# Exponentials of a scale and of its double in one ScalarE operation, from a pair (2 alpha, alpha) that GpSimd writes into the buffer of P

## Chip, cores and metric

The kernel runs on one core of one Trainium2 chip. The metric is the device time of one execution in microseconds; the time of the kernel before is the median of three runs. The profile is of one execution, whose own time is given beside its span.

## What is computed

Two independent parts share the core, and their outputs stand side by side in 1280 columns. Part A is a dilated sliding attention over 2048 positions (32 heads, a window of 8 positions with a step of 2) with its projections. Part B is a state space convolution: a kernel K is made from 640 x 192 complex exponents and convolved with u by FFT.

```python
dt = jnp.exp(log_dt)[:, None]
A = A_re + 1j * A_im
logdA = dt * A
dB = dt * Bc
P = jnp.exp(logdA[:, :, None] * l[None, None, :])          # l = 0 .. 2047
K = jnp.einsum("dn,dnl,dn->dl", Cc, P, dB).real
...
Yf = Uf * Kf[None, :, :, :]                                 # FFT of length 2 L
y = irfft2(Yf) + u * Dskip
```

The change touches only the real part of the exponents: exp(m x alpha) with alpha = dt x A_re, for the multipliers m that the tables need.

## The kernel before

**Tables.** The 640 channels are worked off in five chunks of 128 (`NCH`). In a chunk, P is not made for all 2048 positions l: l is split as 64 x j + 8 x b + a, and exponentials are made for a (0 to 7), 8 b (0 to 56) and 64 j (0 to 31). These are 48 places `e` in the table R (128 partitions, 48 x `NE_R` = 48 x 4 numbers in bf16): places 0 to 7 hold a, 8 to 15 hold 8 b, 16 to 31 hold 64 j for j from 16 to 31, and 32 to 47 hold 64 j for j from 15 down to 0. `R_MULT` (L55) lists the multipliers. In `exps_chunk` (L213 to L223) GpSimd writes ones to the three places with m = 0 (L217, L218), and ScalarE makes the other 45 with one operation each (L222): 192 numbers of alpha in f32, times the scale m, through Exp, to 4 neighbouring numbers in each of 48 groups. R has two buffers, R0 and R1, for even and odd chunks.

The phases come from `trig_half` (L226), once per half chunk: TensorE makes them in PSUM (ps_ph, L247 and L250), and ScalarE takes the sine (L255) into the tables TA and TX. Exp and Sin need different tables of ScalarE, so a table load stands at each turn from one to the other.

**Products.** `small_half` (L265) runs on VectorE, all at L271 but for one scaling at L286. It writes P (a product of R and TA), Q (P times the coefficients cT), F, G, and two tiles X. P and Q are there to make F; after Q is written nothing reads P. P, F and G have one buffer each; Q and the following Y share four buffers with the tag Y. `y_form` (L296) makes Y from F and G, three for each of the two units of a half chunk (L305), and `kgen_unit` (L309) multiplies X and Y on TensorE into ps_k (L318, L323), which ScalarE copies to Ksb (L324).

**FFT.** `fwd` (L327) transforms in two stages on TensorE (ps_f, L337 and L343), with a copy by ScalarE after each of their four parts (A at L338, Sg at L344). It runs for u (`fwd_u`) and for K of the chunk before (`transform`). `products` (L348) multiplies both spectra on VectorE (L358), and `inverse_a` goes back (Z, L375).

**Order.** Every engine works its instructions in program order; a scheduler merges the operations that the functions of `body` (L662) issue into one order per engine, and `keep_in_program_order` and `issue_after` tie some of them. In the loop over chunks (L719) the order of ScalarE from chunk to chunk is: TA and TX of the second half, the coefficients of the next chunk (L206, L207), a table load, the 45 exponentials of the next chunk with copies (Ksb, Z, A, Sg) in between, a table load, TA and TX of the next chunk's first half. From chunk 0 to 1 all 45 stand ahead of A and Sg of `fwd_u`; from 1 to 2 the last 31 stand behind Sg; from 2 to 3 the last 18, and from 3 to 4 the last 12. P of the next chunk waits for its TA. In chunk 0 the exponentials follow right after alpha (L155, fill of chunk 0), beside VectorE's preparation of the phases (L175 to L193). Pools named `prep_...` exist only in this preparation; `tabb` holds P, F, G, X, Y and UD.

GpSimd has little to do: ones into R, descriptors for some loads, and at the start two operations on the coefficients (L209, L210) and a copy (L694). Later it copies a few columns of kT (L481).

Of the kernel before, what the change touches and what calls it, by code (L numbers as in the profile page):

```python
# [10 lines left out]
A = mybir.AluOpType  # L11
ACT = mybir.ActivationFunctionType
AX = mybir.AxisListType
bf16 = mybir.dt.bfloat16
f32 = mybir.dt.float32
# [36 lines left out]
    return F1, F64  # L52


R_MULT = [float(a) for a in range(8)] + [8.0 * b for b in range(8)] + [64.0 * (16 + i) for i in range(16)] + [64.0 * (31 - i) for i in range(16, 32)]  # L55
L1_OF_ROW = [16 + i for i in range(16)] + [31 - i for i in range(16, 32)]


# [23 lines left out]
def inline(nc, arr, name):  # L82
    return nc.inline_tensor(np.ascontiguousarray(arr).astype(np.float32).astype(ml_dtypes.bfloat16), name=name).ap()
# [118 lines left out]
def coefficients(engine, B, c):  # L202

    co = B["cT"][:, c]
    if engine.engine == mybir.EngineType.Activation:
        engine.activation(out=co[:, :, 1], in_=co[:, :, 2], func=ACT.Copy, scale=-1.0)  # L206
        engine.copy(out=co[:, :, 3], in_=co[:, :, 0])  # L207
    else:
        engine.tensor_scalar(out=co[:, :, 1], in0=co[:, :, 2], scalar1=-1.0, scalar2=None, op0=A.mult)  # L209
        engine.tensor_copy(out=co[:, :, 3], in_=co[:, :, 0])  # L210


def exps_chunk(tc, pools, B, c):  # L213
    nc = tc.nc
    R = pools["tab"].tile([128, 48, NE_R, 4], bf16, name="R", tag=f"R{c % 2}")
    src = B["alpha"][:, c].rearrange("p u (q f) -> p (u q) f", f=4)
    nc.gpsimd.memset(R[:, :, 0:16:8, :], 1.0)  # L217
    nc.gpsimd.memset(R[:, :, 47, :], 1.0)  # L218
    for e, m in enumerate(R_MULT):
        if m == 0.0:  # L220
            continue
        nc.scalar.activation(out=R[:, :, e, :], in_=src, func=ACT.Exp, scale=m)  # L222
    return R  # L223


# [122 lines left out]
def products(tc, pools, Sk, Sd, pool, late):  # L348

    nc = tc.nc  # L350
    P1 = pool.tile([128, 32, 32, 4], bf16, name="P1", tag="sp", bufs=3)
    P2 = pool.tile([128, 32, 32, 4], bf16, name="P2", tag="sp", bufs=3)
    fl = lambda t: t.rearrange("p a b c -> p (a b c)")
    nc.sync.dma_start(out=fl(P1[:]), in_=Sd)
    nc.sync.dma_start(out=fl(P2[0:64]), in_=Sd[64:128])
    nc.sync.dma_start(out=fl(P2[64:128]), in_=Sd[0:64])
    for P in (P1, P2):
        ins = nc.vector.tensor_tensor(out=P[:], in0=P[:], in1=Sk[:], op=A.mult)  # L358
        if late:
            tc.keep_in_program_order(ins)  # L360
    return P1, P2, ins


def inverse_a(tc, pools, C, P1, P2, Zd, pool):

    nc = tc.nc
    MM = nc.tensor.matmul
    Z = pool.tile([128, 128, 32], bf16, name="Z", tag="sp", bufs=3)

    def piece(b):  # L370
        ps = pools["psum"].tile([128, 8, 128], f32, name="ps_ia", tag="bank2")
        for j in range(8):
            for w, P in enumerate((P1, P2)):
                MM(ps[:, j], lhsT=P[:, 8 * b + j].rearrange("p k g -> p (k g)"), rhs=C["EA"][:, w, :], start=(j % 4 == 0 and w == 0), stop=(w == 1), skip_group_check=True)
        nc.scalar.copy(out=Z[:, :, 8 * b:8 * b + 8], in_=ps[:].rearrange("p j x -> p x j"))  # L375
        if b == 3:
            nc.sync.dma_start(out=Zd, in_=Z[:].rearrange("p x j -> p (x j)"))

    return [lambda b=b: piece(b) for b in range(4)]
# [11 lines left out]
def fwd_u(tc, pools, C, Sd, c):  # L391

    U = C["U"][:].rearrange("p l (ut c) -> p c l ut", c=NCH)[:, c]
    Su, last = fwd(tc, pools, C, (lambda ut: U[:, :, ut]), 0, pools["fft"])
    tc.nc.sync.dma_start(out=Sd[c], in_=Su[:].rearrange("p a b c -> p (a b c)"))
    return last
# [265 lines left out]
def body(tc, ctx, pools, prm, B_u, B_Dskip, Sd, Zd, UDd, A_x, A_wqkv, A_wo, out_a, out_b):  # L662
    nc = tc.nc
# [12 lines left out]
    R, trig = {}, {}  # L676
    with tc.tile_pool(name="prep_b", bufs=1) as pb, tc.tile_pool(name="prep_c", bufs=1) as pc, tc.tile_pool(name="prep_a", bufs=1) as pa, tc.tile_pool(name="psum_p", bufs=2, space=bass.MemoryType.PSUM) as psp:
        pools.update(prep_a=pa, prep_b=pb, prep_c=pc)
        B, fill = partB_prep(tc, dict(pools, psum=psp), prm)
        fill(0, 1, lambda u: None)  # L680
        Dn = pa.tile([128, 160], bf16, name="Dn")
        dsrc = B_Dskip.rearrange("(g ch) -> g ch", g=4)
        late = tc.keep_in_program_order
        late(nc.sync.dma_start(out=BD[:].rearrange("p a b n -> p (a b n)"), in_=inline(nc, cn["BD"], "c_BD")))
        late(nc.sync.dma_start(out=EA[:].rearrange("p a n -> p (a n)"), in_=inline(nc, cn["EA"], "c_EA")))
        late(nc.sync.dma_start(out=T2[:].rearrange("p a n -> p (a n)"), in_=inline(nc, cn["T2"], "c_T2")))
        for g in range(4):
            late(nc.sync.dma_start(out=Dn[32 * g:32 * g + 32, :], in_=dsrc[g].partition_broadcast(32)))
        coefficients(nc.gpsimd, B, 0)
        R[0] = exps_chunk(tc, pools, B, 0)  # L690
        trig[0, 0] = trig_half(tc, pools, B, 0, 0)
        usrc = B_u[0].rearrange("(l1 l0) (g ch) -> g l1 l0 ch", l0=64, g=4)
        fill(1, NCH, lambda g: late(nc.sync.dma_start(out=U[32 * g:32 * g + 32], in_=usrc[g])))
        nc.gpsimd.tensor_copy(out=Dsb[:], in_=Dn[:].rearrange("p (ut c) -> p c ut", c=NCH))  # L694
# [5 lines left out]
    def transform(c):  # L700
        Sk[c] = fwd(tc, pools, C, (lambda ut: Kb[c][:, ut, :]), 1, fp)[0]

    def unit(c, h, uu, F, G, X, between=lambda: None):
        Ys = [y_form(tc, pools, F, G, uu, k) for k in range(3)]
        between()
        kgen_unit(tc, dict(pools, psum=psg), 2 * h + uu, X, Ys, Kb[c])
        if 4 * c + 2 * h + uu in UD_AFTER:
            times_d(tc, pools, C, UDd, *divmod(UD_AFTER.index(4 * c + 2 * h + uu), 2))
# [10 lines left out]
    for c in range(NCH):  # L719
        Kb[c] = (fp, pools["tabb"])[c % 2].tile([128, 32, 64], bf16, name="Ksb", tag="Ksb")  # L720
        F, G, Xs = small_half(tc, pools, B["cT"][:, c], R[c], *trig[c, 0][:2], 0)
        if c > 0:
            transform(c - 1)
        trig[c, 1] = trig_half(tc, pools, B, c, 1)
        unit(c, 0, 0, F, G, Xs[0])
        if c > 0:
            P1, P2, last = products(tc, pools, Sk[c - 1], Sd[c - 1], fp, True)
            ia = inverse_a(tc, pools, C, P1, P2, Zd[c - 1], fp)
            ia[0]()
        unit(c, 0, 1, F, G, Xs[1])  # L730
        if c > 0:
            for f in ia[1:]:
                f()
        if c < LAST:
            last_u = fwd_u(tc, pools, C, Sd, c if c == 0 else c + 1)
            if c == 0:
                first_u = last_u
        if c == LAST:
            att.open_k()
            for ct in range(5):  # L740
                att.proj_k(0, ct)
            att.k_halo()
        with ExitStack() as order:
            if c > 0:
                order.enter_context(tc.issue_after(last.ins))
            F, G, Xs = small_half(tc, pools, B["cT"][:, c], R[c], *trig[c, 1][:2], 1)
        if c < LAST:
            with tc.issue_after(trig[c, 1][2].ins):
                coefficients(nc.scalar, B, c + 1)
                R[c + 1] = exps_chunk(tc, pools, B, c + 1)  # L750
            trig[c + 1, 0] = trig_half(tc, pools, B, c + 1, 0)
        else:
            att.open_q0()
        with ExitStack() as order:
            if c == 0:
                order.enter_context(tc.issue_after(first_u.ins))
            unit(c, 1, 0, F, G, Xs[0])
        if c == 0:
            fwd_u(tc, pools, C, Sd, 1)
        unit(c, 1, 1, F, G, Xs[1], q_first if c == LAST else lambda: None)  # L760
        if c == LAST - 1:
            att.load_x()
# [45 lines left out]
    def fill(some, n=1):  # L808
        for f in some[0:n]:
            f()  # L810
        del some[0:n]
# [14 lines left out]
    for i0, ni, j0, nj, done in ((0, 128, 2, 3, 0), (128, 128, 2, 3, 1), (256, 128, 0, 4, None), (256, 256, 4, 1, 2), (384, 128, 0, 4, 3)):  # L826
        for w in range(W):
            att.av_step(i0, ni, j0, nj, w)
            if (done, w) in LOADS:
                qr, c = LOADS[done, w]  # L830
# [16 lines left out]
def kernel(  # L847
# [28 lines left out]
    Zd = dpool.tile([NCH, 128, 4096], bf16, name="Zdram")  # L876
    UDd = dpool.tile([NCH, 128, 2048], bf16, name="UDdram")
    body(tc, ctx, pools, prm, B_u, B_Dskip, Sd, Zd, UDd, A_x, A_wqkv, A_wo, out_a, out_b)


# [28 lines left out]
```

## Time and profile before

| | |
|---|---|
| time, median of 3 runs | 439.51 us (439.4 to 442.8) |
| profiled execution, its own time | 438.98 us |
| its span | 437.2 us |
| PE (matmul) busy | 358.4 us, 82% |
| VectorE (DVE) busy | 391.3 us, 89% |
| ScalarE (ACT) busy | 314.0 us, 72% |
| GpSimd (POOL) busy | 44.5 us, 10% |
| mean granted TensorE clock | 0.916 |
| the 225 exponentials (L222) | 59.3 us busy, mean 358 ns of one |
| the 60 products Y (L305) | 102.9 us busy, mean 1751 ns of one |

In the rows of the profile an operation is given with its line in the kernel, its engine, the tile written and the tiles read ("R<-LPC": alpha lies in the tile LPC), and the shapes in partitions x elements. Operations of one engine overlap a little at their ends, so the mean length of one is more than the distance from one to the next. In a timeline the columns are start, length (both in us, from the start of the span), engine, line, operation, tiles, shapes and count; in brackets stands the idle time of the engine ahead of it and what ended that. In rows by window the columns after the window's length are the busy time and the count of instructions of PE, PE's weight loads, DVE, ACT and POOL, then the granted clock, the DMA share and GB/s.

The chunks end, by the first product P of the next one, at 75.72 (chunk 1 begins), 133.35, 184.28 and 233.99 us.

### The profile page before, as it was taken

What the parts mean: (1) busy time and instruction counts of PE and PEld (TensorE: products, weight loads), DVE (VectorE), ACT (ScalarE), POOL (GpSimd) and SP (SyncE); (2) the same over time, 40 slices, a digit from 0 to 9 for tenths busy, and PEclk for the clock granted to TensorE, in tenths of its full rate; (3) what the DMA queues carried; (4) which work ended last, traced back from release to release, by engine and by line L of the source; (5) the groups of instructions that cost most, each with busy time, mean ns of one, the idle gap of its engine ahead of it and who ended that gap; (6) DMA issues with size and microseconds to landing.
All of it is one profiled execution on the core that took longest, in us unless ns stands there. A gap on an engine that the chain in (4) does not pass through costs nothing.

```text
span 437.2 us, 17687 instructions
## 1 busy us (share of the span) xinstructions
PE 358.4 (82%) x8041; PEld 241.1 (55%) x8041; DVE 391.3 (89%) x386; ACT 314.0 (72%) x570; POOL 44.5 (10%) x85
## 2 busy tenths in 40 slices
PE   1397659989886998879778799999899897399995
PEld 0145546866863677556665665545555674134443
DVE  7889999999997999999999989946978989999751
ACT  3974998889999899979997845342858344544663
POOL 7440000000000000000010000400001204102110
PEclk9996577999999898889999899999999999659999
DMA  5569102163233402324079933500210907957343
GB/s 143 186 141 200 18 3 109 39 227 94 99 123 123 97 28 98 144 103 99 27 258 241 236 75 135 178 0 3 67 32 1 265 17 201 228 141 225 96 107 114
DMA packets 45131, 51.62 MB, mean 118 GB/s; under 512 B 31376, under 2 KB 38992, under 8 KB 42368
## 3 DMA queue, kind: packets, MB, share of 16 engines
q1 hardware_dynamic: 41520, 41.41, 35.4%
q0 software_dynamic: 3392, 8.95, 7.0%
q8 instruction: 63, 1.03, 1.0%
q10 hardware_dynamic: 144, 0.12, 0.1%
q14 instruction: 12, 0.10, 0.1%
HBM read 28.03 MB, written 18.35 MB: 106 GB/s over the span
## 4 chain that ended last, share of the span: by engine, by line
PE 49%; ACT 29%; DVE 14%; issue 5%; DMA 1%; SPq 1%; DVEq 0%; ACTq 0%
ACT R L222 10%; ACT A L338 6%; PE ps_k L318 6%; PE ps_ph L247 6%; PE ps_k L323 6%; PE ps_op L420 6%; PE ps_k L470 4%; PE ps_q L488 4%; PE ps_ph L250 4%; ACT Sg L344 4%; PE ps_f L343 4%; PE ps_v L501 2%; DVE prod L521 2%; ACT Z L375 2%; PE ps_o L420 2%
## 5 line engine op out<-in xcount | busy, mean ns | idle before, releaser
L305 DVE TENSOR_TENSOR Y<-F,G 128x3072 bf16<-128x3072 bf16 x60 | 102.9, 1751 | 0.6 <-PE ps_k L323 0.6
L222 ACT ACTIVATE R<-LPC 128x192 bf16<-128x192 f32 x225 | 59.3, 358 | 0.1
L247 PE MATMUL ps_ph<-LPC 128*128 128x256 bf16 (+1 forms) x200 | 41.5, 311 | 17.3 <-DMA LPC<-lo 8.7
L318 PE MATMUL ps_k<-Y,X 128*32 128x64 bf16 x1920 | 47.2, 239 | 7.3 <-DVE Y L305 3.8
L323 PE MATMUL ps_k<-Y,X 64*32 64x64 bf16 x1920 | 43.8, 233 | 3.4 <-issue 3.3
L344 ACT CAST Sg<-ps_f 128x1024 bf16<-128x1024 f32 x40 | 37.6, 1027 | 7.3 <-PE ps_f L343 7.3
L318 PEld LDWEIGHTS <-X 128*32 128x32 bf16 x1920 | 32.1, 117 | 17.4 <-issue 9.0
L343 PE MATMUL ps_f<-A,T 128*128 128x128 bf16 x320 | 27.3, 259 | 14.9 <-ACT A L338 14.2
L338 ACT CAST A<-ps_f 128x1024 bf16<-128x1024 f32 x40 | 37.6, 1036 | 0.7 <-PE ps_f L337 0.6
L271 DVE TENSOR_TENSOR X<-R,TX 128x1536 bf16<-128x1536 bf16 x40 | 36.4, 951 | 0.0
L323 PEld LDWEIGHTS <-X 64*32 64x32 bf16 x1920 | 29.6, 113 | 12.1 <-issue 4.4
L255 ACT ACTIVATE TX<-ps_ph 128x864 bf16<-128x864 int16 (+1 forms) x40 | 31.9, 867 | 5.3 <-DVE X L271 2.5
L343 PEld LDWEIGHTS <-T 128*128 128x128 bf16 x320 | 25.6, 119 | 16.1 <-issue 14.9
L585 DVE TENSOR_TENSOR prod<-v,atp 128x2048 bf16<-128x2048 bf16 (+2 forms) x32 | 31.3, 1018 | 2.0 <-PE ps_o L420 1.8
L255 ACT ACTIVATE TA<-ps_ph 128x768 bf16<-128x768 int16 x40 | 30.6, 822 | 3.4 <-PE ps_ph L250 3.0
L250 PE MATMUL ps_ph<-LPC 128*64 128x128 bf16 (+1 forms) x400 | 29.6, 249 | 0.0
L247 PEld LDWEIGHTS <-LPC 128*128 128x128 bf16 x200 | 15.0, 102 | 25.9 <-issue 19.1
L420 PE MATMUL ps_op<-wo,o 128*128 128x320 bf16 x160 | 28.5, 315 | 0.8 <-ACT o L595 0.4
L358 DVE TENSOR_TENSOR P<-P,Sg 128x4096 bf16<-128x4096 bf16 x10 | 22.9, 2288 | 4.1 <-DMA P<-Sdram 3.2
L250 PEld LDWEIGHTS <-LPC 128*64 128x64 bf16 x400 | 15.2, 118 | 19.1 <-issue 18.9
L611 ACT CAST ob<-ps_op 128x320 bf16<-128x320 f32 x28 | 11.9, 431 | 19.0 <-PE ps_op L420 17.3
L337 PE MATMUL ps_f<-BD,U 128*64 128x128 bf16 x320 | 19.4, 285 | 6.1 <-ACT A L338 3.3
(129 smaller groups left out, 661.2 us busy)
## 6 DMA issues: line engine op xcount, KB each, us to landing
Sdram<-Sg SPq DMA_DIRECT2D x5, 1024.0 KB
P<-Sdram SPq DMA_DIRECT2D x5, 1024.0 KB
P<-Sdram SPq DMA_DIRECT2D x10, 512.0 KB
Zdram<-Z SPq DMA_DIRECT2D x5, 1024.0 KB
Z<-Zdram SPq DMA_DIRECT2D x30, 128.0 KB
U<-in_B_u_dram SPq DMA_DIRECT2D x4, 640.0 KB
UDdram<-UD SPq DMA_DIRECT2D x10, 256.0 KB
out_dram<-ysb SPq DMA_DIRECT2D x32, 80.0 KB
```

What stands on the lines that cost most here:

```text
L222: nc.scalar.activation(out=R[:, :, e, :], in_=src, func=ACT.Exp, scale=m)
L247: MM(o[:, :, 0:32], lhsT=L[:, 0:128], rhs=rhs, start=first, stop=last, skip_group_check=True)
L250: MM(o[64 * hh:64 * hh + 64, :, 32:48], lhsT=L[:, 128:192], rhs=rhs[:, :, 16 * hh:16 * hh + 16], start=False, stop=last, skip_group_check= ...
L255: last = nc.scalar.activation(out=dst[:, qs, e0:e0 + 2 * n, :].rearrange("p q (b e) f -> p b e q f", b=2), in_=words.rearrange("p b (e q f ...
L271: TT = lambda o, a, b, op: V.tensor_tensor(out=o, in0=a, in1=b, op=op)
L305: nc.vector.tensor_tensor(out=Y[:].rearrange("p q (b a) f -> p q b a f", a=8), in0=fa, in1=gb, op=A.mult)
L318: MM(ps[32 * g:32 * g + 32, t], lhsT=X[:, q, 2 - k, :, f], rhs=Ys[k][:, q, :, f], start=(t == 0 and k == 0), stop=False, tile_position=(0, ...
L323: MM(ps[32 * g:32 * g + 32, t], lhsT=X[hb, q, 2 - k, :, f], rhs=Ys[k][hb, q, :, f], start=False, stop=(k == 2), tile_position=(64 * (g // ...
L338: nc.scalar.copy(out=A1[:, :, 32 * b:32 * b + 32].rearrange("p k (j g) -> p k j g", g=4), in_=ps[:].rearrange("p j k g -> p k j g"))
L343: last = MM(ps[:, kk], lhsT=C["T2"][:, 8 * b + kk, :], rhs=A1[:, 8 * b + kk, :], start=(kk % 4 == 0), stop=True, skip_group_check=True)
L344: nc.scalar.copy(out=Sg[:, :, 8 * b:8 * b + 8, :], in_=ps[:].rearrange("p k (j g) -> p j k g", g=4))
L420: self.MM = lambda *a, **k: self.tc.keep_in_program_order(self.nc.tensor.matmul(*a, **k))
```

## The change

Exponentials of m and 2 m are made by one operation where both are needed. Its input is a pair of tiles, `twice`: 2 alpha and alpha side by side; with the scale m the operation gives exp(2 m alpha) and exp(m alpha) at once, to two places of R. Among 1 to 7 and among 8 to 56 the pairs are (1, 2) and (3, 6), and 4, 5 and 7 times the unit stay single; among 64 to 1984 there are ten pairs and eleven singles. That makes 14 pairs of 384 numbers and 17 singles of 192: 31 operations instead of 45. The singles, which read alpha itself, come first.

`twice` is written by two scalings of 192 f32 numbers each. In chunk 0 VectorE does it, into a tile of the preparation. For the chunks 1 to 4 GpSimd does it, into a tile with the tag of P in `tabb`: after the Q of the second half of the chunk before, and ahead of the P of the next chunk, which waits until the pairs were read. On GpSimd the writes stand ahead of the ones for R. In the merged order the pairs stand: from chunk 0 to 1 all ahead of A and Sg; from 1 to 2 all behind Sg; from 2 to 3 and from 3 to 4 two between A and Sg and twelve behind Sg. The order of the other operations is the same but for small moves; in chunk 0 the two scalings on VectorE stand ahead of the first subtraction of the phases (L179).

```diff
-R_MULT = [float(a) for a in range(8)] + [8.0 * b for b in range(8)] + [64.0 * (16 + i) for i in range(16)] + [64.0 * (31 - i) for i in range(16, 32)]
...
-def exps_chunk(tc, pools, B, c):
+def exps_chunk(tc, pools, B, c, engine, twice):
     nc = tc.nc
     R = pools["tab"].tile([128, 48, NE_R, 4], bf16, name="R", tag=f"R{c % 2}")
-    src = B["alpha"][:, c].rearrange("p u (q f) -> p (u q) f", f=4)
+    alpha = B["alpha"][:, c].rearrange("p u w -> p (u w)")
+    for b in range(2):
+        engine.tensor_scalar(out=twice[:, b], in0=alpha, scalar1=2.0 - b, scalar2=None, op0=A.mult)
     nc.gpsimd.memset(R[:, :, 0:16:8, :], 1.0)
     nc.gpsimd.memset(R[:, :, 47, :], 1.0)
-    for e, m in enumerate(R_MULT):
-        if m == 0.0:
-            continue
-        nc.scalar.activation(out=R[:, :, e, :], in_=src, func=ACT.Exp, scale=m)
+    one, two = [], []
+    for places in ({a: a for a in range(1, 8)}, {8 * a: 8 + a for a in range(1, 8)}, {64 * j: j if j > 15 else 47 - j for j in range(1, 32)}):
+        left = sorted(places)
+        while left:
+            m = left.pop(0)
+            e, step = places[m], 0
+            if 2 * m in left:
+                left.remove(2 * m)
+                step = places[2 * m] - e
+            (two if step else one).append((m, e, step))
+    for m, e, step in one + two:
+        src = twice[:].rearrange("p b (q f) -> p q b f", f=4)
+        if step == 0:
+            src, out = alpha.rearrange("p (q f) -> p q f", f=4), R[:, :, e, :]
+        elif step < 0:
+            out = R[:, :, e + step:e + 1:-step, :]
+        else:
+            src, out = src[:, :, ::-1, :], R[:, :, e:e + step + 1:step, :]
+        nc.scalar.activation(out=out, in_=src, func=ACT.Exp, scale=float(m))
     return R
...
-        R[0] = exps_chunk(tc, pools, B, 0)
+        R[0] = exps_chunk(tc, pools, B, 0, nc.vector, pa.tile([128, 2, 192], f32, name="twice"))
...
         if c < LAST:
+            twice = pools["tabb"].tile([128, 2, 192], f32, name="twice", tag="P")
             with tc.issue_after(trig[c, 1][2].ins):
                 coefficients(nc.scalar, B, c + 1)
-                R[c + 1] = exps_chunk(tc, pools, B, c + 1)
+                R[c + 1] = exps_chunk(tc, pools, B, c + 1, nc.gpsimd, twice)
             trig[c + 1, 0] = trig_half(tc, pools, B, c + 1, 0)
```

## The prediction

> **What bounds the kernel now.** I read the page's totals first, then busy time by stage, then the timelines of three engines around the places where R is made.
>
> ```profile
> PE 358.4 (82%) x8041; PEld 241.1 (55%) x8041; DVE 391.3 (89%) x386; ACT 314.0 (72%) x570; POOL 44.5 (10%) x85
> L222 ACT ACTIVATE R<-LPC 128x192 bf16<-128x192 f32 x225 | 59.3, 358 | 0.1
> ...
> 156.00:181.00 25.00, 20.36 (x567) 17.78 (x556) 25.00 (x23) 24.64 (x60) 0.62 (x2) 0.93 0.28 108
> 181.00:208.00 27.00, 23.39 (x639) 15.69 (x639) 27.00 (x24) 23.54 (x35) 0.00 (x0) 0.87 0.32 90
> 208.00:231.00 23.00, 17.89 (x474) 15.16 (x475) 23.00 (x23) 22.98 (x55) 1.78 (x2) 0.93 0.45 162
> ```
>
> VectorE (third group in the rows by window) is busy in every microsecond from 156 to 231. ScalarE (fourth) is nearly as full, so the exponentials are no idle-time work; but only where VectorE waits for ScalarE does a shorter ScalarE shorten the span. Between 40 and 240 us there is one such place, the first product of chunk 2:
>
> ```profile
> 133.35 0.96 DVE L271 TENSOR_TENSOR P<-R,TA 128x1536 bf16<-128x1536 bf16 x1 [3.02 <-ACT TA L255]
> ```
>
> The 3.02 us are all that faster exponentials can win in the chunks. Now GpSimd, which gets a new job. It reads SBUF in only a few instructions, and one falls into dense VectorE work:
>
> ```profile
> 26.92 0.34 POOL L210 COPY cT<-cT 128x192 bf16<-128x192 bf16 x1
> 29.39 0.37 POOL L694 COPY Dsb<-Dn 128x160 bf16<-128x160 bf16 x1
> 279.80 3.98 POOL L481 COPY kT<-kT 128x280 bf16<-128x280 bf16 x1 [5.74 <-ACT kT L471]
> ...
> 275.07 8.42 DVE L305 TENSOR_TENSOR Y<-F,G 128x3072 bf16<-128x3072 bf16 x5
> 286.48 1.30 DVE L518 TENSOR_TENSOR prod<-ql,kT 128x1024 bf16<-128x1024 bf16 x2 [2.99 <-ACT ql L489]
> ```
>
> A copy of 160 to 192 elements takes 0.34 to 0.37 us beside scalings or at the end of VectorE's work (26.42 to 27.60 are four scalings, at 29.50 it stands). The copy of 280 elements took 3.98 us: it began inside the fourth of five Y products, two more began after it (at 280.08 and 281.75), and it ended at 283.78, 0.29 us after the last (275.07 + 8.42 = 283.49), when VectorE stood. The scaling of cT at 25.15 (1.80 us) also ended only 0.55 us after two VectorE products that ran at its start. Memsets, which only write, take 0.42 us under the same load. I read this as: a GpSimd instruction that reads SBUF waits as long as VectorE has products of two tensors back to back.
>
> **The change, part by part.** Exponentials: 45 per chunk become 17 singles and 14 pairs. A single costs 11.49/45 = 0.255 us. No row has 384 elements; the sines of 768 follow each other at (3.16 - 0.82)/3 = 0.78 us, and the line through both gives 0.43 at 384; through the 1024-element casts (0.89 us apart) 0.40; above is 0.51, two singles. I take 0.43, as the sine has the same output pattern: 14 pairs are 6.0 us, and a chunk's set saves 14 x 0.08 = 1.2 us.
>
> Start (chunk 0): ScalarE's exponentials end at 20.1 instead of 21.30. But the two new VectorE operations (0.17 each, from the rows of L177) stand ahead of the pieces of the phase and need alpha, which is written at 9.76, while VectorE gets there at 7.94: it stands for 1.9 us, and has idle time of 1.69 at 15.3 and 1.29 at 29.5 to give back. Taken 0; bounds -1.2 and +2.2.
>
> Chunks 1 to 4: GpSimd writes 2 x 192 elements into P's place. Its first write waits for Q of half 1, the last reader of P. The pairs stand behind these writes on ScalarE, and behind the pairs on the same engine stand the copies of both FFT stages (A, Sg), the table load and TA of the next chunk; TensorE waits for those, with the matmuls of ps_k queued behind its FFT matmuls. A write costs 0.35 (the copies of 160 and 192; upper bound 1.8, the scaling of cT): 0.75 for both with their semaphores. The singles come first, so ScalarE loses little until the pairs. On GpSimd's own queue, R's memsets and at the end the loads of wkq come behind the writes; wkq is first used at 267.9, so its delay is hidden.
>
> Then the question is when VectorE stands. Into chunk 1:
>
> ```profile
> 52.21 4.68 ACT L222 ACTIVATE R<-LPC 128x192 bf16<-128x192 f32 x18
> 57.25 4.16 ACT L222 ACTIVATE R<-LPC 128x192 bf16<-128x192 f32 x16
> 61.31 3.72 ACT L338 CAST A<-ps_f 128x1024 bf16<-128x1024 f32 x4
> ...
> 56.52 1.75 DVE L271 TENSOR_TENSOR Q<-P,cT 128x3072 bf16<-128x3072 bf16 x1
> 72.39 3.42 DVE L305 TENSOR_TENSOR Y<-F,G 128x3072 bf16<-128x3072 bf16 x2
> 75.72 0.95 DVE L271 TENSOR_TENSOR P<-R,TA 128x1536 bf16<-128x1536 bf16 x1
> ```
>
> Q ends at 58.27; VectorE then runs without a gap. ScalarE waits, so A (61.31 before) doesn't come, TensorE stops in its FFT, the Y of the unit are not consumed, and with four Y buffers VectorE stops at the fifth Y, the second of the two at 72.39: 74.06. Now GpSimd writes: 74.8. Pairs: 80.8. From A's start to TA's end it was 61.31 to 75.11, 13.8 us: 94.6, where P of chunk 1 stood at 75.72: **+18.9**. Into chunk 2 (times of before, shifted by what came earlier): FFT copies are ahead of the pairs, so VectorE runs on to P, 130.33; writes 131.1; pairs 137.1; from the table load to P 3.6 us as before (129.74 to 133.35): 140.7 against 133.35, **+7.4**. Into chunk 3 two pairs stand ahead of Sg, so Y again is not consumed: fifth Y 179.72, writes 180.5, two pairs 181.4, Sg's four copies 3.6, twelve pairs 5.2, table to P 3.6: 193.8 against 184.28, **+9.5**. Into chunk 4 the same from 230.65: 244.7 against 233.99, **+10.7**. Later VectorE waits 1.17 us for a load at 256.49; some 0.5 of it is given back. Sum 18.9 + 7.4 + 9.5 + 10.7 - 0.5 = **+46**. The profiled execution has a span of 437.2 and a time of 438.98, 1.8 around the span and 0.5 under the median of 439.51. 437.2 + 46 + 1.8 = **485 us**. Its own range is 475 to 495: a pair at 0.40 or 0.51 moves 56 pairs by -1.7 or +4.5, writes at 1.8 add up to 11, and a stop found earlier takes off several.
>
> The Trainium skill, "SBUF — State Buffer", section "Who interferes with whom", says that a VectorE instruction with two SBUF inputs contends with a GpSimd instruction that reads SBUF, and that whichever issues first holds the shared pair for the whole instruction while the other blocks. That the copy is held agrees with its 3.98 us; but by that rule as written it would have come in at the next VectorE instruction, at 280.08, and the change would cost what the second rival below costs. The copy went past two such places.
>
> **Rivals.**
> - *GpSimd gets some reads in between VectorE's instructions.* For it: the copy's long span alone doesn't show whether it moved in between. Against: after VectorE stopped it still needed 0.29 us, nearly a whole copy. If the two writes need some six instructions after Q (58.3 to 63), pairs end at 69 instead of 61.3, P of chunk 1 comes 7 us late, chunk 2 gives back 1.2, and later writes are done before ScalarE gets to the pairs: +6 to +15, **447 us**.
> - *GpSimd comes in at the next instruction.* Writes done at 59.6, pairs 65.6 instead of 61.31; TA had 0.6 to spare: +3.7. Into chunk 2 ScalarE's path is 1.2 shorter: +2.5, and four later writes hold VectorE for 0.35 each: +3.9, **443 us**. Against: 280.08 and 281.75.
> - *The other side: faster.* GpSimd comes in at once and a pair costs hardly more than a single (0.26), if ScalarE took both scales together: 3.6 us saved per set. Into chunk 1 +1.3; chunk 2's idle time shrinks by up to 3.0; the start wins up to 3.3: -5, **434 us**. It decides from a pair under some 0.3 us; every longer operation of the engine costs in proportion to its elements, which speaks against it.
> - That the set is not as said (31 operations, the pairs last) is excluded by the order of the instructions.
>
> **How the numbers follow.** Waiting until VectorE stands 0.68, some reads in between 0.12, next instruction 0.13, faster 0.04, worse than 495 (the writes slow as well) 0.03. Own range 475 to 495 holds some 0.61; 0.80 needs the two milder cases, so 442 to 495. About 1% is what a measurement of this kernel tells from no change (435.1 to 443.9): the next-instruction case lies mostly inside. Faster 0.04, same 0.11, slower 0.85.
>
> **What would show it.** Right: each GpSimd write of twice, or the first of each pair of them, several to 16 us long or starting when VectorE begins to stand; ScalarE idle before the first pair by some 18 us into chunk 1; VectorE idle for some 18, 7 to 10, 9 and 11 us per chunk; pairs 0.4 to 0.5 apart. Wrong: writes of 0.4 us soon after Q, with VectorE back to back beside them; then the time is near 443. VectorE's busy time should stay near 391.

## The result and the profile after

The changed kernel takes **490.23 us** (median of 6 runs, 479.17 to 494.91) against 440.19 us for the kernel before (6 runs, 438.2 to 442.8). The ratio of the comparison is 1.0915 (95% interval 1.0823 to 1.1007). That ratio uses only executions within 1.5% of the fastest of the same kernel, here 479.17 and 482.48 alone, and by the last experiment the longer ones that it leaves out are the usual course of this kernel. The profiled execution has a span of 488.7 us and a time of 490.53.

First the page of the kernel after: the totals, and the groups of GpSimd's writes, of the pairs and of the products Y (count | busy us, mean ns | idle time of the engine just before, and what ended it).

```profile
PE 365.9 (75%) x8041; PEld 243.3 (50%) x8041; DVE 393.7 (81%) x388; ACT 309.0 (63%) x500; POOL 117.0 (24%) x93
...
L323 DVE TENSOR_TENSOR Y<-F,G 128x3072 bf16<-128x3072 bf16 x60 | 103.1, 1752 | 37.8 <-PE ps_k L341 37.8
L219 POOL TENSOR_SCALAR twice<-LPC 128x192 f32<-128x192 f32 x8 | 72.0, 9010 | 165.3 <-DVE Q L289 137.6
...
L240 ACT ACTIVATE R<-twice 128x384 bf16<-128x384 f32 x70 | 29.7, 518 | 50.1 <-POOL twice L219 50.1
```

VectorE is nearly as busy as before (393.7 us against 391.3; 2.1 of the 2.4 us more lie ahead of the first P and are taken up under the start below). Its products Y are as long as before (1752 ns against 1751), so in the chunks it is not slowed; it stands more. Eight scalings of 192 numbers on GpSimd took 72 us. ScalarE stood 50.1 us for them, VectorE 37.8 us for TensorE. By the timeline of GpSimd:

```profile
60.33 16.87 POOL L219 TENSOR_SCALAR twice<-LPC 128x192 f32<-128x192 f32 x2 [27.68 <-issue]
...
131.10 21.42 POOL L219 TENSOR_SCALAR twice<-LPC 128x192 f32<-128x192 f32 x2 [53.34 <-DVE Q L289]
...
193.40 16.84 POOL L219 TENSOR_SCALAR twice<-LPC 128x192 f32<-128x192 f32 x2 [40.32 <-DVE Q L289]
...
254.73 16.84 POOL L219 TENSOR_SCALAR twice<-LPC 128x192 f32<-128x192 f32 x2 [43.93 <-DVE Q L289]
```

Each pair of writes begins 0.2 us after Q, as soon as P's place is free, and lasts 17 to 21 us. What happens meanwhile is in the rows by window (length, busy time and count of PE, PEld, DVE, ACT and POOL, then granted clock, DMA share, GB/s), and in the timelines of ScalarE and VectorE:

```profile
60.50:76.00 15.50, 0.40 (x8) 0.37 (x7) 15.49 (x16) 0.00 (x0) 15.50 (x1) 0.57 0.05 17
76.00:94.20 18.20, 8.58 (x150) 6.97 (x153) 0.00 (x0) 15.84 (x25) 1.76 (x4) 0.61 0.11 43
```

```profile
77.24 5.89 ACT L240 ACTIVATE R<-twice 128x384 bf16<-128x384 f32 x14 [18.52 <-POOL twice L219]
83.03 3.72 ACT L356 CAST A<-ps_f 128x1024 bf16<-128x1024 f32 x4
```

```profile
94.23 1.76 DVE L323 TENSOR_TENSOR Y<-F,G 128x3072 bf16<-128x3072 bf16 x1 [18.23 <-PE ps_k L341]
95.90 0.95 DVE L289 TENSOR_TENSOR P<-R,TA 128x1536 bf16<-128x1536 bf16 x1
...
162.07 0.96 DVE L289 TENSOR_TENSOR P<-R,TA 128x1536 bf16<-128x1536 bf16 x1 [10.74 <-ACT TA L273]
...
218.07 3.43 DVE L323 TENSOR_TENSOR Y<-F,G 128x3072 bf16<-128x3072 bf16 x2 [9.04 <-PE ps_k L341]
...
279.44 3.43 DVE L323 TENSOR_TENSOR Y<-F,G 128x3072 bf16<-128x3072 bf16 x2 [9.07 <-PE ps_k L341]
```

From 60.5 to 76.0 only VectorE works; ScalarE does nothing at all and TensorE nearly nothing. Then VectorE's buffers are used up and it stops (94.23 - 18.23 = 76.00). The writes end at 77.20, the pairs begin at 77.24, and VectorE stands until the FFT behind the pairs has caught up. Standing of 18.2, 10.7, 9.0 and 9.1 us follows in the four chunks.

### The profile page after: what moved, and what is told of

The parts are those of the page before. It is cut to its first block, busy times and chain, and to the rows that moved or that the text cites. A ratio compares the mean times of both kernels' runs of the same rounds, so it can differ in the third digit from the quotient of the medians.

```text
span 488.7 us, 17626 instructions
## 1 busy us (share of the span) xinstructions
PE 365.9 (75%) x8041; PEld 243.3 (50%) x8041; DVE 393.7 (81%) x388; ACT 309.0 (63%) x500; POOL 117.0 (24%) x93
## 5 line engine op out<-in xcount | busy, mean ns | idle before, releaser
L323 DVE TENSOR_TENSOR Y<-F,G 128x3072 bf16<-128x3072 bf16 x60 | 103.1, 1752 | 37.8 <-PE ps_k L341 37.8
L219 POOL TENSOR_SCALAR twice<-LPC 128x192 f32<-128x192 f32 x8 | 72.0, 9010 | 165.3 <-DVE Q L289 137.6
L265 PE MATMUL ps_ph<-LPC 128*128 128x256 bf16 (+1 forms) x200 | 46.0, 336 | 22.7 <-ACT TA L273 11.6
L240 ACT ACTIVATE R<-twice 128x384 bf16<-128x384 f32 x70 | 29.7, 518 | 50.1 <-POOL twice L219 50.1
L362 ACT CAST Sg<-ps_f 128x1024 bf16<-128x1024 f32 x40 | 37.5, 1024 | 6.8 <-PE ps_f L361 6.8
L268 PE MATMUL ps_ph<-LPC 128*64 128x128 bf16 (+1 forms) x400 | 32.7, 264 | 1.4 <-issue 1.4
L355 PEld LDWEIGHTS <-U 128*64 128x64 bf16 x320 | 18.7, 204 | 23.7 <-issue 23.2
L268 PEld LDWEIGHTS <-LPC 128*64 128x64 bf16 x400 | 16.3, 122 | 24.3 <-issue 24.1
```

Of the source, the lines that this page charges most:

```text
L219: engine.tensor_scalar(out=twice[:, b], in0=alpha, scalar1=2.0 - b, scalar2=None, op0=A.mult)
L265: MM(o[:, :, 0:32], lhsT=L[:, 0:128], rhs=rhs, start=first, stop=last, skip_group_check=True)
L268: MM(o[64 * hh:64 * hh + 64, :, 32:48], lhsT=L[:, 128:192], rhs=rhs[:, :, 16 * hh:16 * hh + 16], start=False, stop=last, skip_group_check= ...
L323: nc.vector.tensor_tensor(out=Y[:].rearrange("p q (b a) f -> p q b a f", a=8), in0=fa, in1=gb, op=A.mult)
L355: MM(ps[64 * ri:64 * ri + 64, j], lhsT=src_fn(8 * b + j), rhs=C["BD"][:, wh, ri, :], start=(j % 4 == 0), stop=True, skip_group_check=True, ...
```

## The experiments

**The same waits, but GpSimd only writes.** For the chunks 1 to 4:

```diff
-        engine.tensor_scalar(out=twice[:, b], in0=alpha, scalar1=2.0 - b, scalar2=None, op0=A.mult)
+        engine.memset(twice[:, b], 0.0) if c > 0 else engine.tensor_scalar(out=twice[:, b], in0=alpha, scalar1=2.0 - b, scalar2=None, op0=A.mult)
```

> The changed kernel with one difference: for chunks 1 to 4 GpSimd writes twice as zeros (a memset of the same 192 f32 numbers) and reads nothing; waits, places and order of all instructions are the same. Left out: the numbers 2 alpha and alpha of these chunks, so the pairs make ones. Theory (a GpSimd instruction that reads SBUF is held while VectorE runs two-tensor products back to back): the writes take 0.3 to 0.4 us each right after Q, the first pair comes about 1 us after Q, VectorE no longer stands for 9 to 18 us per chunk, time 439 to 447. Rival (what costs is P's place, the order of the writes ahead of R's ones, or the pairs themselves): the same waits are there, time 475 to 495.

Measured: 441.73 us beside 440.11 for the kernel before. GpSimd's rows:

```profile
59.11 0.45 POOL L219 MEMSET twice<- 128x192 f32 x2 [26.71 <-DVE Q L289]
...
113.71 0.46 POOL L219 MEMSET twice<- 128x192 f32 x2 [46.84 <-ACT R L240]
```

Both writes together take 0.45 us, and the first pair follows at 59.60. P's place, the order on GpSimd, the pairs, their number and their place are all as in the changed kernel; only the read of alpha is gone, and with it some 48 us. The rival is out.

**GpSimd's scalings added to the kernel before** (the added line is written out as a loop here).

```diff
                 R[c + 1] = exps_chunk(tc, pools, B, c + 1)
+                for b in range(2):
+                    nc.gpsimd.tensor_scalar(out=B["LP"][:, b, :, c, 0:96].bitcast(f32), in0=B["alpha"][:, c + 1], scalar1=2.0 - b, scalar2=None, op0=A.mult)
```

> The kernel before, to which GpSimd gets the two scalings of the next chunk's alpha for each of chunks 0 to 3, written into a dead part of the phases of the chunk; nobody reads the result. Nothing of R waits for them; the ones for R of a later chunk stand behind them on GpSimd. Theory (held as long as VectorE has products back to back, until it stands): with a stand of VectorE of 1 us or more only at 133 and behind 234 in the kernel before, at least one of the first writes lasts 20 us or more, up to some 70; VectorE is not slowed (busy 391, 60 Y at 1.75 us), time 438 to 444. Rival 1 (it comes in between two instructions): each write under 3 us. Rival 2 (both engines slow each other): Y longer than 1.8 us beside the writes.

Measured: 462.18 us, not 438 to 444. The first writes of the four pairs lasted 34.5, 26.5, 4.1 and 30.9 us (both writes of a pair together in the rows), and Y is 1.76 us long, so beside these products the hold is one-sided as expected. The time was wrong because somebody did wait: the phases of the next chunk lie in the same tile, and TensorE's matmuls for them were held behind the write.

```profile
39.48 35.16 POOL L750 TENSOR_SCALAR LPC<-LPC 128x192 f32<-128x192 f32 x2 [10.07 <-DMA LPC<-lo]
...
215.43 31.53 POOL L750 TENSOR_SCALAR LPC<-LPC 128x192 f32<-128x192 f32 x2 [28.61 <-PE ps_ph L247]
```

The row of the waits (us in total, times, longest):

```profile
PE ps_ph L247 <- POOL LPC L750: 19.2, 6, 6.5
```

So in three of the four places the hold again ended only when everything behind it had stopped VectorE. The third write, of 4.1 us, came in at a pause of VectorE of 0.64 us (at 167.97).

**A VectorE instruction with one input behind Q.** In three kernels one instruction was put into `small_half` behind Q of each second half: a sum over 1024 numbers of Q, a scaling of Q by 1.0, and a sum over 128 numbers (shortened: `Q_flat` is Q as 128 x 3072, and `gap` a tile of 128 x 8).

```diff
+    h and V.tensor_reduce(out=gap[:], in_=Q_flat[:, 0:1024].rearrange("p (a b) -> p a b", a=8), axis=AX.X, op=A.add)
```
```diff
+    h and V.tensor_scalar(out=Q_flat, in0=Q_flat, scalar1=1.0, scalar2=None, op0=A.mult)
```
```diff
+    h and V.tensor_reduce(out=gap[:], in_=Q_flat[:, 0:128].rearrange("p (a b) -> p a b", a=8), axis=AX.X, op=A.add)
```

> The changed kernel with one more VectorE instruction behind Q of each chunk's second half: a sum over 1024 numbers of Q into 8 (one input from SBUF), about 1 us, whose result is not used. Theory in its narrow form (products of two tensors hold GpSimd, an instruction with one input does not): the first write of twice, asked for as Q ends, gets in beside the sum and is done within 1 us, the second in it or, if it misses it, held as before; with both in, time 443 to 455 including 5 us for the five sums. In its wide form (anything that VectorE runs without a pause holds it): writes of 16 to 21 us as before and a time of 480 to 495.

> As the kernel with the sum behind Q, but in its place a scaling of Q by 1.0 in place (3072 bf16 numbers, one input from SBUF, about 1 us). Theory A (any VectorE instruction with one input lets GpSimd in): writes of 0.7 to 0.9 us, time 445 to 451. Theory B (a scaling or copy of bf16 in SBUF holds GpSimd as a product does; the scaling of TX, 0.55 us, inside the first held write of the changed kernel speaks for it): writes of 15 to 21 us, time 478 to 500. By the Trainium skill, page SBUF — State Buffer, section Who interferes with whom, a scaling can run in a mode that holds the shared pair and a reduction never does, which is B.

> As the kernel with the sum behind Q, but the sum is over 128 numbers only, some 0.2 us. Theory A (the write gets in only while such an instruction or a stand lasts): the first write is done soon after the sum or not at all, the second is held until VectorE stands, the pair needs both, time 475 to 495. Theory B (once GpSimd has entered, its next instruction goes on before VectorE's next product): both writes done within 2 us of Q, time 441 to 446.

Measured: 447.89, 499.43 and 486.52 us. The long sum, on VectorE and GpSimd:

```profile
60.99 1.21 DVE L297 TENSOR_REDUCE gap<-Q 128x8 f32<-128x1024 bf16 x1
```

```profile
60.77 1.51 POOL L219 TENSOR_SCALAR twice<-LPC 128x192 f32<-128x192 f32 x2 [27.30 <-issue]
```

Both writes are done within 1.5 us, in all four chunks. An instruction of 1.2 us that was added to the busiest engine, five times, saved over 40 us. With the scaling, both writes together:

```profile
59.70 17.74 POOL L219 TENSOR_SCALAR twice<-LPC 128x192 f32<-128x192 f32 x2 [26.81 <-issue]
```

With the short sum, the first write alone and then both together:

```profile
59.38 0.86 POOL L219 TENSOR_SCALAR twice<-LPC 128x192 f32<-128x192 f32 x1 [26.81 <-issue]
```

```profile
59.38 16.39 POOL L219 TENSOR_SCALAR twice<-LPC 128x192 f32<-128x192 f32 x2 [26.81 <-issue]
```

The scaling (0.95 us, one input, bf16) holds GpSimd like a product; the longest of its four first writes took 21.7 us, just over the range expected. So my words "products of two tensors" were too narrow. The Trainium skill, "SBUF — State Buffer", section "Who interferes with whom", lists a `tensor_scalar` among the operations that can take the pair of ports shared with GpSimd, and says that a reduction never contends on trn2; the run with the scaling and the two with a sum agree with it. The short sum (0.28 us) let the first write in, done after 0.86 us; the second, the next instruction on GpSimd, was held for the rest of the 16.39 us. Entry is asked for anew by each instruction.

**The pairs of chunk 0 alone.**

```diff
+    for b in range(2 if c == 0 else 0):
...
+            if c == 0 and 2 * m in left:
```

> Only chunk 0 has its exponentials as pairs, with VectorE's two scalings; the chunks 1 to 4 are as before. Theory: VectorE stands some 1.9 us for alpha before the scalings and this is not given back, so 1.5 to 2.5 us longer than before (440.5 to 442.5). Rival of the prediction's sum (given back in the idle places at 15 and 29 us): within 0.7 us of before.

Measured: 441.5 us (10 runs) against 440.11 (13 runs), ratio 1.0027 (0.9992 to 1.0062). VectorE stands 1.79 us for alpha, and the first P begins at 34.70 instead of 33.87. The time lies in the range expected, but the interval does not exclude nothing at all, and the reason expected is not what the trace shows: the stand was given back, and the 0.83 us come from elsewhere (see the start, below).

**A place of its own, and early.** Pairs for the chunks 2 to 4 only (`pairs`); `twice` lies in the coefficients of the chunk before last, written by GpSimd, or in the second kernel by ScalarE.

```diff
+    pairs = c in (2, 3, 4)
+    if pairs and c > 1:
+        twice = B["cT"][:, c - 2].rearrange("p w s f -> p (w s f)").bitcast(f32).rearrange("p (b w) -> p b w", b=2)
+    for b in range(2 if pairs else 0):
         engine.tensor_scalar(out=twice[:, b], in0=alpha, scalar1=2.0 - b, scalar2=None, op0=A.mult)
```
```diff
+        nc.scalar.activation(out=twice[:, b], in_=alpha, func=ACT.Copy, scale=2.0 - b)
```

> Pairs only for the chunks 2 to 4 (45 singles for 0 and 1), and GpSimd writes twice not in P's place but into the coefficients of the chunk before last, which nobody reads any more; so it may ask as early as it gets there, chunk 2's at about 58 us, 60 us before the pairs are due. Theory (held until VectorE stands, however long): the first write lasts 60 us or more, until VectorE waits for the tables of chunk 2 at 130; that of chunk 3 can slip in at the same stand; that of chunk 4 is held until ScalarE, TensorE and so VectorE have stopped for it. Chunk 2 costs 7, chunk 4 some 10: time 450 to 465. Rival (P's place and the late request were what cost, somewhere in 60 us it comes in): writes under 10 us, time 437 to 441.

> As the one before (pairs for the chunks 2 to 4, twice in the old coefficients), but ScalarE writes twice itself ahead of its singles, at about 0.26 us a write. Nothing of GpSimd is in the way. A set costs 17 x 0.255 + 14 x 0.41 + 0.5 = 10.6 us instead of 11.5: at most some 1 to 2 us of the 3 us for which VectorE waits ahead of chunk 2 can go, the rest is hidden behind VectorE. Theory: 436.5 to 440.5, within 1% of before and maybe 0.3% faster. Rival (pairs that must all stand behind the singles, or 384-element operations, delay the tables): 442 or more.

Measured, with GpSimd: 460.36 us.

```profile
37.00 0.85 POOL L222 TENSOR_SCALAR cT<-LPC 128x192 f32<-128x192 f32 x1 [7.23 <-DVE Q L292]
57.96 18.87 POOL L222 TENSOR_SCALAR cT<-LPC 128x192 f32<-128x192 f32 x1 [20.11 <-DVE Q L292]
81.29 49.37 POOL L222 TENSOR_SCALAR cT<-LPC 128x192 f32<-128x192 f32 x2 [3.89 <-ACT A L359]
135.25 0.86 POOL L222 TENSOR_SCALAR cT<-LPC 128x192 f32<-128x192 f32 x1 [4.04 <-DVE Q L292]
162.38 67.22 POOL L222 TENSOR_SCALAR cT<-LPC 128x192 f32<-128x192 f32 x1 [26.26 <-DVE Q L292]
```

The time is as expected, but by luck, for two misses cancel: chunk 2 was to cost 7 us and cost nothing (its P begins at 131.60, before at 133.35), and chunk 4 was to cost some 10 and cost 21.9 (its P begins 71.6 us after that of chunk 3, at 254.32, instead of 49.7). A long lead doesn't help: chunk 3's writes (81.29) were held until VectorE stood ahead of chunk 2 at 129.5, and the second of chunk 4 (162.38) for 67.2 us, until VectorE had stopped for it, a stand of 18.4 us. But chunk 2's writes were done early, and cost nothing: the one at 57.96 came in where VectorE paused for 0.08 us (at 76.29), the one at 37.00, like the first of chunk 4 at 135.25, came in with VectorE running on, which the theory does not provide for.

With ScalarE as the writer: 438.34 us (12 runs) against 439.22 (17 runs), ratio 0.9968 (0.9935 to 1.0002). VectorE's stand ahead of chunk 2 is 2.23 us instead of 3.02. This is the best that the pairs brought: a gain of the size reckoned, not told apart from none.

**The changed kernel again, three times**, unaltered, for the difference between its executions.

> The changed kernel once more, unaltered, for a second profile beside the first, whose TensorE clock was low (0.874). Theory: GpSimd's first writes are held 16 to 21 us again and end about 0.55 us after VectorE stands; if the part of the span that the prediction's sum lacks (51 against 46) comes from TensorE's clock in and behind the stands, P of the chunks 1 to 4 begin earlier in a profile with a higher clock, and the span lies near 478 to 483. Rival (a step of the sum was too short by itself): the same places and a span near 488 whatever the clock.

> The changed kernel unaltered, a third profile. In the first (span 488.7) all four first writes were held, in the second (480.6) the one into chunk 4 got in right behind Q and that chunk cost nothing. Theory (the spread of this kernel's times is the number of holds, some 8 to 11 us each, 18 for the one into chunk 1): a span of 486 to 493 goes with four held writes, 476 to 483 with three (one of the last three missing), 468 to 474 with two, or with three where the one into chunk 1 is missing. Rival (the spread is TensorE's clock): four held writes with a span near 480, or three with one near 489.

> A fourth profile of the changed kernel, with the same expectations: 486 to 493 with four held writes, 476 to 483 with three, 468 to 474 with two; rival: no such relation.

Measured: profiles with spans of 480.6, 488.3 and 492.4 us. In the last two all four first writes were held for 16 to 21 us, as in the first profile (488.7). In that of 480.6 three were held, and into chunk 4 both writes came in at once; GpSimd, and VectorE beside it:

```profile
254.40 1.85 POOL L219 TENSOR_SCALAR twice<-LPC 128x192 f32<-128x192 f32 x2 [43.85 <-DVE Q L289]
```

```profile
254.12 0.56 DVE L289 TENSOR_TENSOR G<-G 128x768 bf16<-128x768 bf16 x1
254.59 1.11 DVE L289 TENSOR_TENSOR F<-Q 128x1536 bf16<-128x1536 bf16 x1
255.62 0.69 DVE L289 TENSOR_TENSOR G<-G 128x768 bf16<-128x768 bf16 x1
```

F took 1.11 instead of 0.95 us, G 0.69 instead of 0.55: VectorE gave way for some 0.15 us twice, and chunk 4 cost +0.8 us instead of +11.6. I had ascribed the low time to TensorE's clock, and the span expected for that (478 to 483) came, but not for that reason: P of the chunks 1 to 3 begin no earlier than in the first profile (96.25, 162.44 and 223.20 against 95.90, 162.07 and 223.44), and at nearly the same mean clock (0.885 against 0.889) the third profile has 488.3 us. The number of holds fits all four profiles, though only one of them has three, and it is the one that the theory was made from. Timed beside the kernel before, the changed kernel gave a ratio of 1.1084 (1.1026 to 1.1143).

## Why the prediction was right, point by point

Forecast 485 us, measured 490.2; faster, the same and the milder cases did not come. By the places at which P of each chunk begins, in the first profile after against that before (span 437.2):

| step | forecast | measured |
|---|---|---|
| start, P of chunk 0 (35.77 against 33.87) | 0 | +1.9 |
| into chunk 1 (95.90 against 75.72) | +18.9 | +18.3 |
| into chunk 2 (162.07 against 133.35) | +7.4 | +8.5 |
| into chunk 3 (223.44 against 184.28) | +9.5 | +10.4 |
| into chunk 4 (284.78 against 233.99) | +10.7 | +11.6 |
| behind it | -0.5 | +0.7 |
| sum | +46 | +51.5 |

*Held until VectorE stands:* right in 15 of the 16 places of the four profiles. In chunk 1 of the first VectorE was to stop at 74.06, plus the 1.9 of the start 75.96; it stopped at 76.00. The chain behind it was right too: ScalarE idle 18.5 us ahead of the first pair, TensorE standing in its FFT, the fifth Y as the stop into chunks 1, 3 and 4 and P into chunk 2.

*The start* is the term most mis-sized: taken as 0, inside its bounds of -1.2 and +2.2, and measured at +1.9. The doubt was about VectorE's stand for alpha (1.9 reckoned; 2.27 in the changed kernel, 1.79 with chunk 0 alone), but that was given back as the prediction took it: the idle place at 15 us is gone, the one at 29 us is 0.58 instead of 1.29, and VectorE's idle time from 7.9 us to the first P adds up to 3.6 us before and 3.7 after. The two scalings cost 0.17 us each, as reckoned. The other 1.5 us, for which the sum had no term, are two operations of VectorE that became longer: a cast into `hi` (0.85 instead of 0.54 us) and this scaling, before and after:

```profile
13.91 0.55 DVE L181 TENSOR_SCALAR tr<-tr 128x768 f32<-128x768 f32 x1
```

```profile
16.79 1.78 DVE L180 TENSOR_SCALAR tr<-tr 128x768 f32<-128x768 f32 x1
```

Beside it GpSimd now writes its ones for R in four memsets one behind the other, of which the first and the last are:

```profile
16.96 0.44 POOL L220 MEMSET R<- 128x384 bf16 x1
...
17.88 0.28 POOL L221 MEMSET R<- 128x192 bf16 x1
```

The scaling ends at 18.57, 0.41 us after the last of them. Before, three of the four memsets fell into VectorE's idle time at 15 us. The scaling takes 1.78 us in all nine profiles with pairs in chunk 0 and 0.55 to 0.64 us in the four without. So at the start GpSimd seems to hold VectorE, the other way round; this is read from the rows, and no run moved the memsets alone. With chunk 0 alone it is the same two operations and the two scalings, less 1.1 us of idle time: P comes 0.83 us later.

*A write at 0.35 us* was too low. Two come 1.2 us after VectorE's stop (76.00 to 77.20), not 0.75: the first ends after 0.55, the second takes 0.68. The copies that I took it from move bf16, these f32; no run shows whether that is the reason. It makes 0.4 us in each chunk.

*A pair at 0.43 us:* measured (5.89 - 0.52)/13 = 0.413. 14 pairs took 5.9 us instead of 6.0.

*Into chunk 2:* the stand of 10.74 us is 1.2 for the writes, 5.9 for the pairs and 3.6 from the table load to P, as worked out, against 3.0 before. Of the 1.1 us beyond the forecast's step some 0.4 are the writes; the rest is the Y behind P of chunk 1, which waits 1.42 us for ps_k instead of 0.57, and the sum had no term for it. In the chunks 3 and 4 it is 14.4 us from VectorE's stop to P, forecast 14.1; the rest there are short stands of some 0.5 us at the products of the spectra. *Behind it*, VectorE's wait of 1.17 us for a load, of which 0.5 was to be given back, grew to 1.71.

*The loads of wkq* came out at 271.53 behind the writes and are first used at 312.0: hidden, as said. Before, their first use is at 259.8 (L479), not at 267.9, which is the second group that reads them (L470). One more reading was off without touching the argument: the copy of kT at 279.80 began inside the third of the five Y, not the fourth; two more did begin after it.

*"Next instruction"*, the second rival, is what happened in one of the four places of the 480.6 us profile. Its price was rightly small; I had it as all or nothing, and it is a matter of each entry. *Some reads in between* fell: a held write ends 0.53 to 0.56 us after VectorE's last instruction, in all profiles, and the short sum shows a whole write done or none. *Faster* fell with the price of a pair, and because ScalarE is not what VectorE waits for but ahead of chunk 2. With the reads gone (441.73) and with ScalarE as the writer (438.34) the pairs are worth under 1%.

*The first to issue holds the shared pair for its whole instruction:* so the Trainium skill has it in "SBUF — State Buffer", section "Who interferes with whom", and by it the write enters at the next instruction. That was so for four writes (both into chunk 4 in the profile of 480.6 us, and those at 37.00 and 135.25 us with `twice` in the old coefficients), and not for the others, where the hold went on over up to 60 instructions. What decides is open. The first write at each such entry was asked for 0.19 to 0.23 us ahead of VectorE's next instruction; held ones were asked for just as far ahead (0.19 to 0.23 in the first profile).

## What to carry to other kernels

Before work is moved to an idle GpSimd, ask whether it reads SBUF and what VectorE runs beside it: next to an engine that is full of two-tensor products or bf16 scalings such a read may wait until VectorE stops, and if VectorE in the end needs its result, everything has to run dry first. Look in the old trace for the longest GpSimd instruction that reads; one row of 3.98 us told it here. A short row would have proved nothing: in three of the other profiles the same copy, asked for in a pause of VectorE or 0.2 us ahead of one, took 0.41 to 0.48 us. An operation saved on an engine is worth only the time for which somebody waits for that engine, and here that was 3.0 us in the chunks.

## What the runs showed of the hardware that I had not expected

- Pauses of VectorE as short as 0.08 us, or one 0.28 us sum, let a waiting write in; VectorE's instructions otherwise begin some 0.08 us before the one ahead has ended and leave no pause.
- Of 34 writes asked for beside running VectorE work with neither pause nor sum at hand, 30 were held, for 4.1 to 67 us, and 4 came in at the next instruction, at some 0.15 us of VectorE's time each. I found nothing in the traces that tells them apart.
- GpSimd can be in VectorE's way too: a scaling of VectorE of 768 f32 numbers took 1.78 instead of 0.55 us beside four memsets of GpSimd. Beside the two-tensor products in the chunks memsets changed nothing (in the kernel before, a Y at 65.27 us with two of them beside it is 1.75 us long).
- The spans of the changed kernel spread with the number of holds: 480.6 us in the one profile with three, 488.3 to 492.4 in the three with four.
